# Bucketed attention with two gated layers on one core: first head's maxima by a product, hash products in two parts, zero products in the first waits, a new written sequence

## The chip, the cores and the metric

The kernel runs on one core of a Trainium2 chip. The metric is the time of one execution in device microseconds. The core has a matrix engine (PE in the profile, with its weight loads as PEld), three engines that work on whole tiles (DVE, ACT, POOL) and SP, which here only issues transfers. ACT issues some transfers too; SP and ACT each have a queue of their own, in which a transfer that has to wait holds up everything behind it.

## The reference

Three layers follow each other. The first is attention in which a query sees only the keys of its own hash bucket; the second is a gated layer (`moe`), the third a layer with one of eight experts for each token (`moe2`). The change is in the first.

```python
q_bits = (np.einsum('bhsd,dk->bhsk', q, proj) > 0)     # 6 bits, k likewise
q_bucket = np.sum(q_bits * powers, axis=-1)
mask = q_bucket[:, :, :, None] == k_bucket[:, :, None, :]
scores = np.where(mask, scale * q @ k.T, -1e9)
scores = scores - np.max(scores, axis=-1, keepdims=True)
attn = np.exp(scores); attn = attn / (np.sum(attn) + 1e-09)
out = attn @ v                 # 2 x 8 heads, 768 positions, 64 wide, float32
```

## The kernel before

**Work.** The sixteen heads are taken two at a time: eight pairs `i`, with heads `j` 0 and 1 of each. For a pair, q and k are loaded (`l`), turned by six PE transposes each (`tt`, line 636), and split into a leading part (`tc`, ACT, line 645) and a rest (`td`, DVE, line 658; for the last pair two products and an ACT copy, `tl`). Products with the hash matrix PRJ give the signed dots (`pk`/`pb`, line 667), one DVE comparison makes bits of them (`bi`, line 672; for the first pair four smaller ones, `bh`, line 688). Leading parts, rests and bits are copied into the operand tile T of each head, by transfers (`d0`, `d1`, `d2`, `e2`), for the first pair partly by ACT and POOL copies (`c0`, `c1`).

**Maxima and scores.** For each head six blocks of 128 queries are multiplied with all keys, bits included (`sm`, line 720), and DVE takes the row maxima (`sx`, line 728). The maxima are turned by a PE transpose (`mk` step 0, line 735), limited from below on DVE (step 1, line 738) and sent by a transfer on ACT's queue into one row of T (step 4, line 748); steps 2 and 3 mark the queries without a key. With that row in T the score products (`sc`, line 757) come out with the maximum already subtracted. ACT takes the exponential (`ex`, line 765), POOL the rest of it in 16 bits (`pl`, line 776), and three products a block with v give the output (`pv`, lines 792 to 794; `pu` adds the unmatched queries). `va`, `vx`, `vs` scale v, `sv` and `mvm` make its mean, `ho` divides.

**Start.** DVE zeroes PRJ (`prz`, line 910), fills rows and constants (`rows`, lines 553 to 567), then constants from the identity tile (`vm1`, lines 581 to 586; `nid`, line 912), then PRJ (`prj`, lines 541 to 550, when `proj` has landed). PE makes two columns from the rows (`cols`, line 572). The identity tile is made by POOL ahead of everything. POOL zeroes T (`z`) and other tiles and makes constants (`const`).

**Order.** `ORDER` holds one string for each engine (PE, ACT, DVE, POOL, SP), and each engine executes its steps in just that order. `Plan.order` only merges the five strings with the dependencies; the costs in `add(...)` enter there. PSUM has three large buffers ("S") for `tt`, `pb`, `sm` and `sc`; k and q of one pair have one raw buffer each, so the next pair's load waits for this pair's `tt`. In the kernel before, the loads of pair 1 and of its v also wait for the first pair's bits `d1.0.0`:

```python
add(SP, 1300, ("l", i, nm), load_qk, (i, nm), [("l", i - 1, nm)] + [("d1", 0, 0)] * (i == 1), ...)
add(SP, 1270, ("lv", i), load_v, (i,), [("lv", i - 1)] * (i > 0) + [("d1", 0, 0)] * (i == LV0), ...)
```

Of the kernel before, what the change touches and what calls it, by code (L numbers as in the profile page):

```python
# [1728 lines left out]
```

## Time and profile before

| | |
|---|---|
| three runs | 786.21, 787.86 (median), 791.44 us |
| profiled execution, own time | 787.57 us |
| its span, first to last instruction | 785.9 us |
| busy in the span | PE 740.8, PEld 623.6, DVE 464.5, POOL 425.1, ACT 377.5 us |
| mean granted clock of PE | 0.971 |

The span lacks 1.7 us of the execution's own time. Busy time of PE counts a product from its issue to its modelled end, and products overlap. Attention takes the first 244 us of the span, and the gated layers the rest. In the rows, `x6` is a count, a bracket gives the idle time of the engine just before the row and what ended it, and an engine's name with q (SPq, ACTq) is its transfer queue. The granted clock is 1.00 for 2.4 GHz and 0.50 for 1.2 GHz; the record has its first change at 19.5 us.

### The profile page before, as it was taken

The page shows a single profiled execution, that of the slowest core. Times are in us where ns is not written, and L with a number is a line of the kernel's source. Part 1 is how long each engine was busy: PE and PEld are TensorE (multiplying, and loading weights), DVE is VectorE, ACT ScalarE, POOL GpSimd, SP SyncE. Part 2 cuts the span into 40 slices and gives each one's busy share as a digit, 9 for nine tenths or more (in the row PEclk, how much of TensorE's full clock was granted, in tenths as well). Part 3 has the DMA queues.
Part 4 walks back from the last instruction along what each step waited for, and adds up shares of the span by engine and source line. Part 5 has one row for each costly group of instructions (what it writes and reads, how often), then busy time and mean ns, then how long its engine had stood idle before and what let it go on. Part 6 is the DMA issues. An engine that isn't in the chain of part 4 may idle for free.

```text
span 785.9 us, 14028 instructions
## 1 busy us (share of the span) xinstructions
PE 740.8 (94%) x5322; PEld 623.6 (79%) x5322; DVE 464.5 (59%) x869; ACT 377.5 (48%) x612; POOL 425.1 (54%) x378
## 2 busy tenths in 40 slices
...
GB/s 110 205 171 163 152 109 118 114 142 130 122 30 81 108 161 107 164 158 81 1 55 1 0 44 12 14 67 1 80 160 338 335 289 220 218 180 181 23 25 21
DMA packets 109235, 92.17 MB, mean 117 GB/s; under 512 B 45699, under 2 KB 90851, under 8 KB 109164
## 3 DMA queue, kind: packets, MB, share of 16 engines
...
## 4 chain that ended last, share of the span: by engine, by line
PE 81%; DVE 6%; DMA 6%; issue 3%; SPq 1%; ACT 1%; POOL 1%; ACTq 0%; POOLq 0%; DVEq 0%
PE pg L1084 23%; PE pg L1564 11%; PE pss L757 7%; PE psm L720 4%; PE po L1138 4%; PE po L1140 4%; PE po L1139 4%; PE po L1578 3%; PE po L1576 3%; PE po L1577 3%; DMA T<-bits 2%; PE po L792 2%; PE po L793 2%; PE po L794 2%; PE pt L339 1%
## 5 line engine op out<-in xcount | busy, mean ns | idle before, releaser
L776 POOL TENSOR_TENSOR Pl<-Pe 128x768 f16<-128x768 f32 x90 | 133.4, 1503 | 41.3 <-ACT Pe L765 36.8
L456 POOL TENSOR_TENSOR wgl<-r,wgh 128x512 fp32r<-128x512 f32 x64 | 83.5, 1310 | 79.6 <-ACT wgh L466 73.8
L765 ACT ACTIVATE Pe<-pss,ebias 128x768 f32<-128x768 f32 x96 | 84.5, 901 | 76.3 <-PE pss L757 47.7
L728 DVE TENSOR_REDUCE m<-psm 128x1 f32<-128x768 f32 x96 | 90.4, 953 | 34.8 <-PE psm L720 33.1
L757 PE MATMUL pss<-T 128*128 128x256 f32 (+1 forms) x384 | 88.6, 363 | 2.6 <-DMA T<-mT 2.3
L757 PEld LDWEIGHTS pss<-T 128*128 128x128 f32 x384 | 67.1, 198 | 17.5 <-issue 3.4
L1103 POOL TENSOR_TENSOR wol<-wy_o,woh 128x512 fp32r<-128x512 f32 x36 | 48.8, 1358 | 57.8 <-ACT woh L466 57.8
L1103 POOL TENSOR_TENSOR wgl<-wy_g,wgh 128x512 fp32r<-128x512 f32 x29 | 39.0, 1344 | 75.8 <-ACT wgh L466 69.7
L456 DVE TENSOR_TENSOR wvl<-r,wvh 128x512 fp32r<-128x512 f32 x64 | 48.6, 759 | 48.2 <-ACT wvh L466 45.1
L1564 PE MATMUL pg<-xh,wgh 128*128 128x256 f32 x256 | 73.2, 287 | 0.7 <-ACT xh L342 0.7
L1564 PE MATMUL pg<-xh,wgl 128*128 128x256 f32 x256 | 72.5, 283 | 0.0
L1564 PE MATMUL pg<-xl,wgh 128*128 128x256 f32 x256 | 72.5, 283 | 0.0
L1116 DVE TENSOR_TENSOR si<-pg,si 128x512 f32<-128x512 f32 x30 | 20.7, 689 | 78.8 <-PE pg L1084 76.3
L720 PE MATMUL psm<-T 128*128 128x512 f32 x192 | 56.4, 388 | 8.3 <-DMA T<-bits 6.6
L792 PE MATMUL po<-VS,Pe 128*128 128x65 f16 x576 | 62.1, 196 | 0.0
L1103 POOL TENSOR_TENSOR wvl<-wy_v,wvh 128x512 fp32r<-128x512 f32 x29 | 40.2, 1388 | 40.2 <-ACT wvh L466 36.2
L1084 PE MATMUL pg<-xh,wgh 128*128 128x512 f32 x144 | 57.6, 400 | 4.3 <-ACT wgh L466 4.3
L794 PE MATMUL po<-VS,Pl 128*128 128x65 f16 x576 | 61.0, 193 | 0.5 <-POOL Pl L776 0.5
L793 PE MATMUL po<-VS,Pe 128*128 128x65 f16 x576 | 61.5, 195 | 0.0
L466 ACT CAST wgh<-r 128x512 fp32r<-128x512 f32 x64 | 39.7, 620 | 42.0 <-PE pg L1564 31.0
L1138 PE MATMUL po<-woh,hh 128*128 128x512 f32 (+1 forms) x148 | 58.8, 397 | 0.1
L792 PEld LDWEIGHTS <-Pe 128*128 128x128 bf16 x576 | 52.7, 97 | 7.6 <-issue 6.0
...
## 6 DMA issues: line engine op xcount, KB each, us to landing
r<-in_moe_w_dram SPq DMA_DIRECT2D x128, 256.0 KB
...
```

The costliest lines, as they stand in the source:

```text
L456: eng.tensor_tensor(out=lo, in0=y, in1=r32(hi), op=ALU.subtract)
L720: nc.tensor.matmul(pm[:, c], Tj[:, 0, 1, t * P:(t + 1) * P], Tj[:, 0, 0, c], start=True, stop=True)
L728: v_.tensor_reduce(out=d["m", j][:, t:t + 1], in_=d.pop(("pm", n)), axis=AX.X, op=ALU.max)
L757: nc.tensor.matmul(pss[:, c], Tj[:, a, 0, ks], Tj[:, a, 1, c], start=a == 0, stop=a == 1)
L765: nc.scalar.activation(d["p", j][0][:, kb], d.pop(("s", n)), AF.Exp, bias=ebias, scale=1.0 / math.sqrt(D))
L776: eng.tensor_tensor(out=Pl[:, kb], in0=Pe[:, kb], in1=leading(Pe, kb), op=ALU.subtract)
L792: nc.tensor.matmul(po, leading(Pe, kb)[:, ts], vf[:, 0], start=t == 0 and kb == 0, stop=False, skip_group_check=True)
L793: nc.tensor.matmul(po, leading(Pe, kb)[:, ts], vf[:, 1], start=False, stop=False, skip_group_check=True)
L1084: nc.tensor.matmul(pg, w_[:, dsl], x_[:, d], start=n == 0, stop=n == 3 * KD - 1)
L1103: nc.gpsimd.tensor_tensor(out=lo, in0=Y[(f, kind)], in1=r32(hi), op=ALU.subtract)
L1138: nc.tensor.matmul(pos[c, t][:, cols], d["hh"][:, tsl], wh[:, cols], start=first, stop=split, skip_group_check=split)
L1564: nc.tensor.matmul(ph, w_[:, dsl], x_[:, d], start=n == 0, stop=n == 3 * KD - 1)
```

## The change

It does nine things, all in attention.

1. `load_pj`: one transfer on ACT's queue, a broadcast over two halves, in place of one on SP and one on ACT.
2. The hash columns move by one, so that the row of maxima is the first of its group (partition 64 or 0), where one instruction can write it.
3. The first head's maxima: `row_first` limits them into column 64 of six zeroed blocks MZ (DVE, `mz.0.0`), multiplies each with a copy of the identity (PE, six products, `mz.0.1`), and copies row 64 of the result into T in two pieces (DVE 512 and ACT 256 elements, `mz.0.2`, `mz.0.3`). Steps 1 and 4 of `mk.0.0` go. MZ, the identity copy and the zeros lie in a part of `T[1][1]`, zeroed by POOL (`zz`) and DVE (`iz`); pair 1's `d2.1.1`, which writes there, waits for all of them.
4. The first pair's hash products in two parts: the two with the leading part (`ph`) right after `tc`, the one with the rest (`pk`, `pb`) after `td`.
5. Zero products of 128x512 (`WARM`): 4 ahead of `cols`, 4 and 3 ahead of `tt.0.k` and `tt.0.q`, 6 ahead of `sm.0.0`. `cols` now waits for `iz` too.
6. `TDA = (1, 4)`: pair 1's rests by two products each and an ACT copy, not on DVE.
7. The loads of pair 1 and of its v no longer wait for `d1.0.0`.
8. The planner's costs for transfers change, and a PE step that waits for a PE step no longer waits out a signal's time in it.
9. All five strings of `ORDER` are written anew, to the end of attention.

```diff
-LV0 = 1
+WARM = {("cols",): 4, ("tt", 0, "k"): 4, ("tt", 0, "q"): 3, ("sm", 0, 0): 6}
-TDA = (4,)
+TDA = (1, 4)
 ORDER = (
-    "cols tt.0.k tt.0.q pk.0 pb.0 sm.0.0 sm.0.4 sm.0.3 sm.0.1 vx.0.1 sm.0.5 sm.0.6 sm.0.2 mk.0.0.0 tt.1.k sm.0.9 sm.0.8 tt.1.q sc.0.0 sc.0.5 sm.0.10 "
-    "tt.2.k pb.1 sc.0.2 sm.0.11 sm.0.7 tt.2.q vx.1.1 mk.0.1.0 sc.0.1 sm.1.0 sm.1.3 vx.0.5 sm.1.1 sc.0.6 sc.0.4 sm.1.5 sc.0.7 vx.1.5 sc.0.11 sm.1.6 sc.0.3 "
+    "cols tt.0.k tt.0.q ph.0.0 pk.0 ph.0.1 pb.0 tt.1.k tl.1.k sm.0.0 sm.0.5 tt.1.q sm.0.2 tl.1.q sm.0.3 sm.0.1 sm.0.4 pb.1 mz.0.1 mk.0.0.0 sm.0.6 sm.0.10 "
+    "sm.0.7 sc.0.0 sm.0.11 vx.0.1 sm.0.9 sc.0.2 sm.0.8 sc.0.3 vx.1.1 sc.0.4 mk.0.1.0 sm.1.0 sc.0.5 sm.1.6 sc.0.1 vx.0.5 sm.1.3 tt.2.k sm.1.11 vx.1.5 "
...
-    "d1.1.0 ex.0.2 tc.2.q mk.0.1.4 ex.0.1 d1.1.1 vs.0.0 ex.0.6 ex.0.4 ex.0.7 ex.0.11 ex.0.3 ex.0.9 ex.0.10 va.1.0 ex.0.8 mk.1.0.4 mr.0.1 vs.1.0 d1.2.0 "
-    "tc.3.k mr.0.3 d1.2.1 mk.1.1.4 ex.1.0 va.1.1 ex.1.5 va.1.2 tc.3.q ex.1.6 ex.1.9 va.1.3 ex.1.8 ex.1.3 ex.1.2 ex.1.4 ex.1.1 ex.1.7 tc.4.k ex.1.10 tc.4.q "
+    "pj l.0.k l.0.q tc.0.k c0.0.0.0 tc.0.q c0.0.1.1 va.0.0 c0.0.0.1 tc.1.k td.1.k d1.0.1.1 tc.1.q td.1.q c0.0.1.0 va.0.2 va.0.1 mz.0.3 d1.1.0 d1.1.1 "
+    "ex.0.0 va.0.3 ex.0.2 ex.0.3 ex.0.4 mk.0.1.4 ex.0.5 ex.0.1 vs.0.0 tc.2.k tc.2.q vs.1.0 ex.0.6 ex.0.10 ex.0.8 va.1.0 mr.0.1 ex.0.7 ex.0.9 mr.0.3 "
+    "mk.1.0.4 va.1.1 va.1.2 ex.0.11 d1.2.0 d1.2.1 ex.1.0 tc.3.k ex.1.2 ex.1.4 mk.1.1.4 tc.3.q ex.1.1 va.1.3 ex.1.5 ex.1.6 ex.1.10 ex.1.3 ex.1.7 ex.1.8 "
...
-    "prz rows vm1 nid prj bc td.0.k td.0.q bh.0.0.0 bh.0.1.0 bh.0.0.1 bh.0.1.1 sx.0.0 sx.0.3 vx.0.0 sx.0.4 sx.0.5 sx.0.1 sx.0.2 sx.0.6 mk.0.0.1 vx.0.2 "
+    "vm1 rows iz nid prz prj td.0.k bc td.0.q bh.0.1.0 bh.0.0.0 bh.0.0.1 bh.0.1.1 sx.0.0 sx.0.5 sx.0.2 sx.0.3 sx.0.1 sx.0.4 vx.0.0 mz.0.0 bi.1 sx.0.6 "
+    "mz.0.2 sx.0.10 sx.0.7 sx.0.11 sx.0.9 mk.0.0.2 vx.1.0 sx.0.8 vx.1.2 vx.0.2 vx.1.3 vx.0.3 mk.0.1.1 sx.1.0 vx.0.4 sx.1.6 vx.1.4 vx.0.6 mk.0.1.2 sx.1.3 "
...
-    "ho.5.1.2 sx.7.1 n5.2 vs.7.1 sx.7.11 mk.7.0.2 mk.7.0.1 sx.7.10 sx.7.7 sx.7.9 n5.3 sx.7.8 mk.7.1.2 ho.6.0.0 mk.7.1.1 ho.6.0.1 pl.7.0 w0.v.2 ho.6.0.2 "
-    "w0.v.3 w0.v.4 pl.7.4 ho.6.1.0 pl.7.6 pl.7.2 ho.6.1.1 ho.6.1.2 pl.7.10 pl.7.8 ho.7.0.0 ho.7.0.1 ho.7.0.2 w0.g.2 w0.g.3 w0.g.4 w0.v.6 w0.g.6 ho.7.1.0 "
+    "mk.6.1.2 vs.7.1 sx.7.2 sx.7.6 mk.7.0.2 mk.7.0.1 sx.7.8 sx.7.7 sx.7.9 sx.7.10 sx.7.11 ho.6.0.0 ho.6.0.1 ho.6.0.2 pl.7.0 w0.g.2 mk.7.1.1 w0.g.3 w0.g.4 "
+    "mk.7.1.2 ho.6.1.0 ho.6.1.1 ho.6.1.2 pl.7.2 pl.7.6 pl.7.4 w0.v.2 pl.7.10 pl.7.8 w0.v.3 w0.v.4 ho.7.0.0 ho.7.0.1 ho.7.0.2 w0.v.6 ho.7.1.0 w0.g.6 "
...
-    "ev.0 z.0.0 z.0.1 ut0 z.1.0 c1.0.0.1 c1.0.1.0 c1.0.1.1 z.1.1 c1.0.0.0 const sv.0.2 pl.0.0 sv.0.0 mk.0.0.3 sv.0.3 pl.0.5 sv.0.1 pl.0.2 pl.0.1 pl.0.4 "
+    "z.0.1 c1.0.0.0 ut0 zz z.0.0 z.1.1 z.1.0 c1.0.1.1 sv.0.1 ev.0 c1.0.1.0 c1.0.0.1 sv.0.2 ev.1 const sv.0.0 sv.0.3 pl.0.2 mk.0.0.3 pl.0.0 pl.0.4 pl.0.3 "
...
-    "l.0.k.0 pj.0 l.0.q.0 lv.0 e2.0.0 d1.0.1.0 e2.0.1 lv.1 l.1.k l.1.q lv.2 l.2.k lv.3 l.2.q d0.1.0 lv.4 d0.1.1 d2.1.1 d2.1.0 lv.5 l.3.k lv.6 d0.2.0 l.3.q "
+    "l.0.k.0 l.0.q.0 lv.0 l.1.k l.1.q lv.1 d1.0.1.0 l.2.k lv.2 e2.0.0 e2.0.1 lv.3 d0.1.0 d0.1.1 l.2.q lv.4 d2.1.1 lv.5 l.3.k lv.6 d2.1.0 d0.2.0 l.3.q lv.7 "
...
+        def idle_zero():
+            v_.memset(r32(spare[:, 0, 0:256]), 0.0)
+
+        def max_zero():
+            nc.gpsimd.memset(r32(MZ), 0.0)
+            nc.gpsimd.tensor_copy(identr, ident)
+
+        def keep_warm(dst, *key):
+            for _ in range(WARM.get(key, 0)):
+                nc.tensor.matmul(dst[:, 0:512], idle[:, 0:P], idle, start=True, stop=True)
...
+        def dots_first(a, part):
+            if part == 0:
+                st[0]["pd", a] = bank("pd")
+            pd = st[0]["pd", a]
+            hi, lo, w = ((1, 0, 1), (2, 3, 0))[a]
+            for c in pieces:
+                for n in range(2 - part):
+                    nc.tensor.matmul(pd[:, c], PRJ[:, w, n], st[0]["hl"][:, lo if part else hi, c],
+                                     start=(part, n) == (0, 0), stop=part == 1, skip_group_check=True)
...
+        def row_first(step):
+            d = st[0]
+            if step == 0:
+                v_.tensor_scalar(out=MZ[:, :, 64], in0=d["m", 0], scalar1=-PEN / 2, scalar2=None, op0=ALU.max)
+            elif step == 1:
+                d["pz"] = bank("pz")
+                for t in range(NT):
+                    nc.tensor.matmul(d["pz"][:, t * P:(t + 1) * P], MZ[:, t], identr, start=t % 4 == 0, stop=t in (3, NT - 1),
+                                     skip_group_check=True)
+            else:
+                c = pieces[step - 2]
+                dst, src = T[0][0][64:65, 0, 1, c], d["pz"][64:65, c]
+                v_.tensor_copy(dst, src) if step == 2 else nc.scalar.copy(dst, src)
...
-        add(PE, 580, "cols", mask_cols, (), ("rows",), -99, "V")
+        add(PE, 580, "cols", mask_cols, (), ("rows", "iz"), -99, "V")
...
-                    add(SP, 1300, ("l", i, nm), load_qk, (i, nm), [("l", i - 1, nm)] + [("d1", 0, 0)] * (i == 1),
+                    add(SP, 1300, ("l", i, nm), load_qk, (i, nm), [("l", i - 1, nm)],
...
-            add(SP, 1270, ("lv", i), load_v, (i,), [("lv", i - 1)] * (i > 0) + [("d1", 0, 0)] * (i == LV0), MLT[b] + LV[i % HP], bw=1970)
+            add(SP, 1270, ("lv", i), load_v, (i,), [("lv", i - 1)] * (i > 0), MLT[b] + LV[i % HP], bw=1850)
```

## Rows read from the trace of the kernel before

**Rows 1.** Busy time by stage: us, PE, PEld, DVE, ACT, POOL, PEclk, DMA share, GB/s
```profile
40.00:50.00 10.00, 6.30 (x19) 5.15 (x20) 4.87 (x7) 3.47 (x5) 3.75 (x4) 0.67 0.63 131
50.00:60.00 10.00, 10.00 (x48) 7.21 (x48) 6.78 (x11) 6.65 (x9) 8.04 (x7) 0.99 1.17 218
...
200.00:210.00 10.00, 10.00 (x106) 8.73 (x106) 5.44 (x8) 5.48 (x7) 5.79 (x5) 0.83 0.52 168
```

**Rows 2.** The chain that ended last, first 60 us: start, us, what
```profile
19.17 4.55 DMA kraw<-in_k_dram
...
35.70 1.07 DVE bits L672
...
37.66 5.91 DMA T<-bits
...
43.70 1.62 PE psm L720 x4
```

**Rows 3.** Timeline, first 5 us: start, us, engine, line, what
```profile
0.89 0.06 DVE L251 MEMSET ebias<- 128x1 f32 x1 [0.89 <-PEq L1713]
...
2.62 1.00 PE L572 MATMUL pc<-one,rowc 1*128 1x1 f32 x4 [2.62 <-DVE one L564]
...
2.91 1.37 POOL L577 MEMSET T<- 64x1536 f32 x1
3.00 0.16 DVE L581 TENSOR_TENSOR diag<-ident 38x6 f32<-38x6 f32 x1 [0.27 <-POOL ident masks.py:199]
...
3.22 1.28 DVE L586 CAST VB<-ident 38x6 f16<-38x6 f32 x4
```

**Rows 4.** Timeline, 5 to 36 us: the same products early and late, and the path to the scores
```profile
5.25 1.51 PE L636 MATMUL pt<-ident,kraw 128*128 128x128 f32 x6 [1.62 <-DMA kraw<-in_k_dram]
...
9.90 4.21 PE L667 MATMUL pd<-HL,PRJ 128*128 128x512 f32 x12 [0.71 <-DVE HL L658]
...
16.67 0.96 DVE L728 TENSOR_REDUCE m<-psm 128x1 f32<-128x768 f32 x1
...
23.90 0.76 ACTq L748 DMA_DIRECT2D T<-mT  x1
...
27.70 1.54 PE L636 MATMUL pt<-ident,qraw 128*128 128x128 f32 x6 [1.05 <-DVE m L728]
...
28.90 2.91 PE L757 MATMUL pss<-T 128*128 128x512 f32 x8
...
33.29 2.36 PE L667 MATMUL pd<-HL,PRJ 128*128 128x512 f32 x12
```

**Rows 5.** Groups on DVE, first 16 us, forms apart: busy us, mean ns, idle before
```profile
L688 DVE TENSOR_SCALAR T<-pd,bc 13x768 fp32r<-13x768 f32 x2 | 2.2, 1080 | 1.2 <-PE pd L667 1.2
...
L658 DVE TENSOR_TENSOR HL<-pt,HL 128x768 fp32r<-128x768 f32 x2 | 1.9, 958 | 0.2 <-ACT HL L645 0.2
...
L910 DVE MEMSET PRJ<- 128x512 f32 x1 | 0.5, 485 | 0.1
```

**Rows 6.** Groups on ACT, first 50 us, forms apart
```profile
L645 ACT CAST HL<-pt 128x768 fp32r<-128x768 f32 x6 | 4.8, 799 | 13.0 <-PE pt L636 12.0 <-DMA qraw<-in_q_dram 0.9
...
L679 ACT CAST T<-HL 64x768 fp32r<-64x768 f32 x4 | 3.3, 825 | 5.6 <-POOL onesb L308 5.6
```

**Rows 7.** Busy time of two short stretches, columns as in rows 1
```profile
8.00:10.00 2.00, 1.29 (x7) 0.89 (x5) 1.71 (x7) 1.24 (x2) 0.00 (x0) 1.00 0.04 8
...
20.00:22.00 2.00, 0.93 (x4) 0.60 (x4) 1.86 (x3) 0.00 (x0) 0.00 (x0) 1.00 1.28 219
```

**Rows 8.** What PE waited for, 150 to 270 us: us in total, times, longest
```profile
PE pg L1084 <- ACT wgh L466: 4.3, 2, 3.8
```

**Rows 9.** Timeline, 190 to 206 us: ACT's queue and the scores behind it
```profile
195.72 4.77 ACTq L709 DMA_DIRECT2D T<-bits  x4
...
199.82 2.36 PE L757 MATMUL pss<-T 128*128 128x512 f32 x8 [2.29 <-DMA T<-mT]
```

**Rows 10.** Timeline, 62 to 65 us: pair 1's first score products
```profile
63.98 0.93 PE L757 MATMUL pss<-T 128*128 128x512 f32 x4
```

More of the change, by code (lines that the diff above doesn't have):

```diff
@@ L188, in order @@
                 heapq.heappush(events, (end + self.WAIT[e], 1, n))
+                if e == PE:
+                    heapq.heappush(events, (end, 2, n))
             if not events:
@@ L195, in order @@
                     continue
-                done += 1
-                for b in steps[n][7]:
-                    room[b].append(self.slots.get((self.taker(n, b), b), 0))
+                if ended == 1:
+                    done += 1
+                    for b in steps[n][7]:
+                        room[b].append(self.slots.get((self.taker(n, b), b), 0))
                 for m in after[n]:
+                    if (steps[n][0] == PE == steps[m][0]) != (ended == 2):
+                        continue
                     left[m] -= 1
@@ L516, in attention @@
         T = [[ea.tile([P, 2, 2, S], F32R, name=f"T{s}{j}") for j in range(2)] for s in range(TB)]
+        spare = T[1][1][:, 1]
+        idle, identr = r32(spare[:, 0, 0:256]).bitcast(BF16), spare[:, 0, 256:256 + P]
+        MZ = spare[:, 1].rearrange("p (t c) -> p t c", t=NT)
         VS = [tp.tile([P, NT, 2, 2 * D + 2], F16, name=f"VS{i}") for i in range(2)]
@@ L534, in attention, with load_pj @@
         vsc = [tp.tile([P, 1], F32, name=f"vsc{g}") for g in range(len(scaled))]
-        def load_pj(j):
-            (nc.scalar if j else nc.sync).dma_start(pj[64 * j:64 * j + 64, 0], proj)
+        def load_pj():
+            nc.scalar.dma_start(pj[:, 0], proj.unsqueeze(0).to_broadcast((2, D, NB)))
         def prj():
@@ L557, in mask_rows @@
                     c0 = row_of(j, w)
-                    v_.memset(rowc[:, 0, c0:c0 + MR], SPEN)
-                    m0 = c0 + NB if w == 0 else c0
+                    v_.memset(rowc[:, 0, c0 + 1:c0 + NR], SPEN)
+                    m0 = c0 + 1 + NB if w == 0 else c0 + 1
                     v_.memset(rowc[:, 0, m0:m0 + NB], -SPEN)
@@ L562, in mask_rows @@
                     if w == 1:
-                        v_.memset(rowc[:, :, c0 + MR:c0 + NR], -1.0)
+                        v_.memset(rowc[:, :, c0:c0 + 1], -1.0)
             v_.memset(one1, 1.0)
@@ L570, in mask_cols @@
             pc = ps_v.tile([P, 512], F32, name="pc", tag=plan.tag("V"))
+            keep_warm(pc, "cols")
             for i in range(2):
@@ L718, in smax @@
             pm = bank("psm")
+            keep_warm(pm, "sm", i, n)
             for c in pieces:
@@ L905, in first_hi @@
             W0[kind] = split_hi(Y[(0, kind)], kind)
-        for j in range(2):
-            add((SP, ACT)[j], 620, ("pj", j), load_pj, (j,), (), -997, bw=20)
+        add(ACT, 620, "pj", load_pj, (), (), -1999, bw=-1500)
+        add(DVE, 170, "iz", idle_zero, (), (), -1000)
+        add(POOL, 900, "zz", max_zero, (), [("z", 0, 1)], -90)
         add(DVE, 325, "prz", lambda: v_.memset(r32(PRJ), 0.0), (), (), -98)
-        add(DVE, 2000, "prj", prj, (), [("pj", 0), ("pj", 1), "prz"], -97, lock=True)
+        add(DVE, 2400, "prj", prj, (), ["pj", "prz"], -97, lock=True)
         add(DVE, 120, "nid", lambda: v_.tensor_scalar(out=nident, in0=ident, scalar1=-1.0, scalar2=None, op0=ALU.mult), (), (), -90, lock=True)
         add(DVE, 1200, "rows", mask_rows, (), (), -99)
-        add(PE, 580, "cols", mask_cols, (), ("rows",), -99, "V")
+        add(PE, 580, "cols", mask_cols, (), ("rows", "iz"), -99, "V")
         add(DVE, 150, "bc", lambda: v_.tensor_copy(bc, st[0].pop("pc")[:, 0:2]), (), ("cols",), -99, "", "V")
@@ L975, in attention @@
                     for w, nm in enumerate("kq"):
-                        add(ACT, 750, ("c0", i, j, w), place_first, (j, 0, w), [("tc", i, nm)], r0 + PT[n][1] + 0.1 + 0.01 * j)
-                        add(POOL, 1200, ("c1", i, j, w), place_first, (j, 1, w), [("tc", i, nm) if w == 0 else ("td", i, nm)], -99)
+                        add(ACT, 830, ("c0", i, j, w), place_first, (j, 0, w), [("tc", i, nm)], r0 + PT[n][1] + 0.1 + 0.01 * j)
+                        add(POOL, 830, ("c1", i, j, w), place_first, (j, 1, w), [("tc", i, nm) if w == 0 else ("td", i, nm)], -99)
@@ L988, in attention @@
+                add(ACT if i < QA else SP, 1650, ("d1", i, j), place, (i, j, 1), [("bi", i)] + war, r0 + PT[n][3] + 0.01 * j, bw=-2200 if i < QA else 240)
+                add(SP, 1270, ("d2", i, j), place, (i, j, 2), hl + war + ([("fz", 0)] + ["cols" if len(key) == 1 else key for key in WARM]) * ((i, j) == (1, 1)), r0 + PT[n][4] + 0.01 * j, bw=4400)
             add(None, 0, ("fh", i), None, (), [("pk", i)] * (i == 0) + [("pb", i)] + [(d, i, j) for d in ("d0", "d2") for j in range(2)], 0, "", "HL")
@@ L1005, in attention @@
                 ring = ACT if i < QA else SP
-                for m, (e, ns) in enumerate(((PE, 110), (DVE, 270), (DVE, 270), (POOL, 180), (ring, 640))):
-                    add(e, ns, ("mk", i, j, m), setm, (i, j, m), [("mk", i, j, (0, 0, 0, 2, 1)[m])] + (["ut0"] + [("pu", i - NUR // 2, j)] * (i >= NUR // 2)) * (m == 2) if m else red, pr + 0.001 * (m in (2, 3)),
-                        ("V", "MK", "", "", "")[m], "", bw=0 if m < 4 else -1800 if i < QA else 20)
-                add(None, 0, ("fv", i, j), None, (), [("mk", i, j, 1), ("mk", i, j, 2)], 0, "", "V")
@@ L1010, in attention @@
-                add(None, 0, ("fm", i, j), None, (), [("mk", i, j, 0)], 0, "", "M")
-                add(None, 0, ("fk", i, j), None, (), [("mk", i, j, 4)], 0, "", "MK")
+                for m, (e, ns) in enumerate(((PE, 110), (DVE, 270), (DVE, 270), (POOL, 180), (ring, 760))):
+                    if (i, j) == (0, 0) and m in (1, 4):
+                        if m == 1:
+                            add(DVE, 140, ("mz", i, 0), row_first, (0,), red + ["zz"], pr)
+                            add(PE, 360, ("mz", i, 1), row_first, (1,), [("mz", i, 0)], pr, "S")
+                            add(DVE, 640, ("mz", i, 2), row_first, (2,), [("mz", i, 1)], pr)
+                            add(ACT, 450, ("mz", i, 3), row_first, (3,), [("mz", i, 1)], pr)
+                            add(None, 0, ("fz", i), None, (), [("mz", i, 2), ("mz", i, 3)], 0, "", "S")
+                        continue
+                    add(e, ns, ("mk", i, j, m), setm, (i, j, m), [("mk", i, j, (0, 0, 0, 2, 1)[m])] + (["ut0"] + [("pu", i - NUR // 2, j)] * (i >= NUR // 2)) * (m == 2) if m else red, pr + 0.001 * (m in (2, 3)),
+                        ("V", "MK", "", "", "")[m], "", bw=0 if m < 4 else -1700 if i < QA else 20)
@@ L1012, in attention @@
+                first = (i, j) == (0, 0)
+                top = ("fz", i) if first else ("mk", i, j, 4)
+                add(None, 0, ("fv", i, j), None, (), [("mk", i, j, 2)] if first else [("mk", i, j, 1), ("mk", i, j, 2)], 0, "", "V")
+                add(None, 0, ("fm", i, j), None, (), [("mk", i, j, 0)] + [("mz", i, 0)] * first, 0, "", "M")
+                if not first:
+                    add(None, 0, ("fk", i, j), None, (), [("mk", i, j, 4)], 0, "", "MK")
                 for m in range(NT):
```

30 lines of the change are left out of this document (15 added, 15 removed), and 86 rows, old and new, of the table ORDER.

## The prediction

> **What bounds the kernel now.** I read the windows first. From 50 us on PE is busy for nearly all of every ten microseconds until the end of attention, at the full clock; in the ten before that it is not: 6.30 us busy, at a mean clock of 0.67 [rows 1]. So what attention gains is what its start gains: work that reaches the full stage earlier ends earlier, and what is added there counts one for one. The chain of waits says what holds the start: not the arithmetic of the first head, but pair 1. Its k leaves late and lands 4.55 us after its issue at 19.17; its bits are made at 35.70; their transfer takes 5.91 us, and only at 43.70 do pair 1's maxima products begin [rows 2]. I therefore take that moment, the first `sm.1`, as the mark by which both kernels are compared, and follow the new order to it on the trace's own time axis.
>
> **The first head: later.** DVE now begins with `vm1`, which waits for the identity; before, that wait ended at 3.00, after two small memsets and one T memset on POOL [rows 3]. In the new order one T memset stands there, so I put it at 2.7. The four small casts of `vm1` took until 4.5 beside a 1.37 us POOL memset [rows 3]; POOL now stands still until `tc.0.k`, so I give the casts the 0.16 us of the small addition beside them [rows 3], and `vm1` 0.65 us: 3.4. `rows` took 1.2 us before: from DVE's first instruction at 0.89 to the release of `cols` at 2.62 [rows 3], less the PRJ memset of 0.485 [rows 5]; `iz` is half such a memset. So DVE frees `cols` at 4.9, not at 2.62. Only then does PE start, and its order is fixed: four zero products, `cols` (1.0 us [rows 3]), four zero products, and then k's transposes, whose data landed at 5.25 [rows 4]. A zero product has no row; the nearest is the hash product of the same width: twelve of them, nine 512-column widths, took 4.21 us early and 2.36 late [rows 4], so 0.26 to 0.47 us for one. I take 0.47, since PE has been idle, and the transposes at 1.51 us early [rows 4]: 4.9 + 3.8 + 1.0 + 1.5 = 11.2 if the low level lasts; as the level may rise on the way, I take 10.5 for the end of `tt.0.k`, against 6.8 before. The zero products hide nothing there, they stand in the way. `proj` on ACT's queue and the columns moved by one I cost at nothing: DVE reaches `prj` at about 5.6 and needs some 2.5 us for it, and the first hash product cannot start before `tc.0.k` at 11.3, so 3 us cover it; without that cover its lateness would go into `ph` one for one.
>
> From 10.5: `tc.0.k` 0.80, `c0` 0.83, `tc.0.q` 0.80 [rows 6] to 13.0, `td.0.q` 0.96 [rows 5] to 14.0. The hash products in two parts pay here: the leading parts run during `tc` and `td`, so that a third of them is left after `td`; but four bit comparisons of 1.08 us [rows 5] follow on DVE anyway, so this is worth about 0.7 us. The second of them needs `z.0.0`, which POOL now reaches after `c1` (0.82), `ut0` (0.8), `zz` (0.9, half a T memset and a copy): at 15.2 with its 1.37. The comparisons end at 17.4 for the first head; six zero products lie ahead of `sm.0.0`, of which half are hidden: first reduction at about 18.9, against 16.67 [rows 4]. The start of the reductions loses 2.2 us.
>
> **The maxima by a product: nothing.** Before, mT left at 23.90 and the scores began at 28.90, but what they waited for was not it: PE stood behind q's transposes of pair 1, which waited for a buffer that a reduction freed at 27.70 [rows 4]. In the new order the six reductions end at 24.8 and `mz.0.0` at 25.0, but `bi.1` (1.08) and `sx.0.6` (0.96) stand ahead of the copy `mz.0.2`. The copy has no row: between 0.16 (38x6 [rows 3]) and 1.08 us (13x768 [rows 5]); I take 0.72 by its 512 columns. With `bi.1` ending at 26.5, `sc.0.0` begins at 28.2, and I count the exchange itself at 0; its bounds are -0.7, by the two starts of the scores, and +1 if `mz.0.3` comes late behind `va` on ACT.
>
> **Pair 1: earlier.** Its k leaves when `tt.0.k` ends, at 10.5 instead of shortly before 19.17 [rows 2], into transfer engines that moved 8 GB/s from 8 to 10 us [rows 7]. With 0.7 us of issue and the 4.55 us of before [rows 2] it lands at 15.8, q at 17.5. Both are turned between the first head's products; the rests come from two products and an ACT copy of 0.80 each, and `pb.1` is done at about 25.4. `bi.1` ends at 26.5 instead of 36.8 [rows 2]. ACT then issues four bit transfers of 0.8 us without a break; with the 5.91 us of landing [rows 2] counted from the second, the bits are there at 33. On DVE, head 1's remaining reductions (five of 0.96, one copy 0.72) after 28.2 end at 33.7, and PE's order has `mk.0.1.0` ahead of `sm.1.0`. Two paths end together: `sm.1.0` at 34.0 against 43.70, a gain of 9.7 us.
>
> Not yet done at the mark are pair 2's transposes, 1.5 us in the early rate, which the kernel before had behind it; the number of score products done is four in both. That leaves 8.2. What the mark does not show: at 43.70 PE had stood for 4 us and ran at half clock to 50 us; if it does not fall this time, up to half of those 6.5 us, 3.3, come on top [rows 1]; I take 0, as reductions and exponentials feed PE there.
>
> **The end of attention.** The first gate weight is now converted ahead of the last output steps. PE waited for it twice, 3.8 us at the longest [rows 8], of which 0.9 right at the change of layer; I take that 0.9, and keep 0 and 2 as ends. For the rest of the new sequence I have no term: its work is the same, and its waits can go either way by some 4 us, as the stall at 195 to 204 us shows [rows 9].
>
> **Sum.** Against the profiled execution, 787.57 us: -9.7 + 1.5 - 0.9 = -9.1, so 778.5 us. That execution lies 0.3 below the median shown.
>
> **Rivals.** First, the transfers become the bound. With both loads of pair 1 pulled ahead, SP's order has 22 blocks of 393 KB up to `d2.1.0`, three more than before, which `sc.1.0` needs. At 219 GB/s [rows 7] that is 39.5 us, from 2.3 us on and with 5 us of forced gaps: 47, against a need at about 54, the mark plus the 20 us that lay between it and pair 1's first scores at 63.98 [rows 10]. At the 131 GB/s of the stage from 40 to 50 us [rows 1] it would be 73; halfway, at 175 GB/s, 57 plus a little to land, a wait of 4: 782.5 us. For it: the chain runs over three such landings [rows 2]; against it: the 131 stands for a stage in which nothing was queued. The Trainium skill, "DMA: Bandwidth & Descriptors", section "Issuing engines are not separate DMA queues", says that transfers from SP and ACT end on the same 16 engines and interleave; by that, bits on ACT's queue would get no path of their own beside the loads. The trace agrees: the bits took 5.91 us beside the loads [rows 2].
>
> Second, the clock stays low through the first head. All of `tt.0`, `ph`, `pb.1` then runs at the early rates: `tt.0.k` 0.7 later, q's transposes and three zero products 1.3, six zero products 1.2 (each by the early less the late price), and of the 1.9 that `pb.1` grows by 0.4 uncovered: 3.6 us, 782.1. For it: the products at 9.90 still took 4.21 us, though PE had done k's transposes from 5.25 on [rows 4]. The Trainium skill, "TensorE: Matmul & The Clock Gate", section "What's actually happening", has the slow level as the default, which activity releases; by that the zero products would bring the full rate by q's transposes. The trace agrees with the default, in that these early rows are slow; none of its stretches shows work on zeros.
>
> Third, slower: ACT's queue. Where four bit transfers are issued in a row (4.77 us), the maxima wait behind them and PE's scores stand for 2.29 us [rows 9], after which the clock is down for some 3.4 us (0.83 over ten [rows 1]), at half worth: 4 us in all. The new ACT order has such rows for pairs 1 and 2 and splits pair 7's, which speaks against it; but each pair has the maxima on this queue. It decides from the third such stall on; with four, 16 - 9 = +7: 794.6 us.
>
> Fourth, more: no half clock from 34 us on (-3.3) and no stall at 195 us: 773 or below.
>
> **Chances.** Forecast 0.45, transfers 0.20, low clock 0.12, ACT's queue 0.09, more 0.14. The range from 770 to 789 leaves out the slower case and little else. A measurement of this kernel can tell about 1%, 7.9 us. Below 780: three in five of the forecast (0.28), the fourth case and a little of the others: 0.47. Above 795.7: 0.07. The rest, 0.46, is within 1%.
>
> **What would show it.** `cols` at about 5 and `tt.0.k` ending near 10.5 in the timeline; first reduction near 19; k of pair 1 issued near 10.5; scores near 28; first `sm.1` near 34; PE full from about 40 in the windows. Wrong if the first transposes are not late, if `sm.1` stands behind bits beyond 38, or if PE shows new waits between 60 and 240 us.

## The result, and the profile after

The changed kernel takes 777.29 us (median of four, 776.77 to 779.23), the kernel before 787.04 in the same runs (784.98 to 791.44): 9.75 us less, ratio 0.987 with an interval from 0.983 to 0.992. The profiled execution took 777.31 us, its span is 775.6 us, PE's mean clock 0.981. The forecast was 778.5.

First the windows, columns as in [rows 1], which the first, second and last line answer:

```profile
40.00:50.00 10.00, 10.00 (x96) 7.65 (x97) 9.49 (x14) 7.83 (x12) 8.24 (x7) 1.00 1.07 203
50.00:60.00 10.00, 9.38 (x139) 8.14 (x139) 7.94 (x13) 5.42 (x9) 8.72 (x10) 1.00 0.80 170
150.00:160.00 10.00, 7.27 (x114) 5.97 (x112) 9.58 (x12) 3.61 (x4) 9.13 (x8) 0.99 0.55 114
160.00:170.00 10.00, 9.79 (x99) 8.72 (x100) 7.14 (x19) 5.43 (x7) 2.89 (x2) 0.84 0.46 101
200.00:210.00 10.00, 9.71 (x142) 8.33 (x141) 7.67 (x10) 5.52 (x7) 8.35 (x7) 1.00 0.01 2
```

From 40 to 50 us PE is now busy throughout at the full clock (6.30 us at 0.67 before), and the stretch around 200 us runs at 1.00 instead of 0.83. But from 150 to 170 us there is a hole of 2.7 us and a stretch at half clock that the kernel before does not have: it had 1.00 there, and 9.24 and 10.00 us busy.

Then the timeline of the changed kernel; it answers [rows 2 to 4], and its last three lines are the hole:

```profile
4.84 1.89 PE L596 MATMUL pc<-T 128*128 128x512 bf16 x4 [4.84 <-DVE T L588]
6.66 1.01 PE L584 MATMUL pc<-one,rowc 1*128 1x1 f32 x4
7.60 1.89 PE L596 MATMUL pt<-T 128*128 128x512 bf16 x4
9.28 1.49 PE L660 MATMUL pt<-ident,kraw 128*128 128x128 f32 x6
10.56 1.49 PE L596 MATMUL pt<-T 128*128 128x512 bf16 x3
...
10.80 1.23 SPq L629 DMA_DIRECT2D kraw<-in_k_dram  x2
...
11.84 1.38 PE L660 MATMUL pt<-ident,qraw 128*128 128x128 f32 x6
...
14.05 4.22 POOL L600 MEMSET T<- 64x1536 f32 x3
...
15.57 0.82 PE L660 MATMUL pt<-ident,kraw 128*128 128x128 f32 x6
...
17.82 1.47 PE L596 MATMUL psm<-T 128*128 128x512 bf16 x6
...
19.67 2.69 DVE L763 TENSOR_REDUCE m<-psm 128x1 f32<-128x768 f32 x3 [0.19 <-PE psm L755]
...
26.00 0.78 PE L792 MATMUL pz<-T 128*128 128x128 f32 x6
...
27.36 4.00 ACTq L743 DMA_DIRECT2D T<-bits  x4
...
29.11 1.00 PE L806 MATMUL pss<-T 128*128 128x512 f32 x4 [0.20 <-DVE T L797]
...
35.13 0.27 PE L770 MATMUL pT<-ident,m 128*6 128x128 f32 x1
...
154.96 4.31 POOL L825 TENSOR_TENSOR Pl<-Pe 128x768 f16<-128x768 f32 x3
...
155.23 4.07 DVE L377 TENSOR_SCALAR nri<-nrb 128x4 int32<-128x4 int32 x1
...
160.21 2.93 PE L806 MATMUL pss<-T 128*128 128x512 f32 x8 [2.94 <-DVE m L763]
```

PE begins at 4.84 with zero products and turns k from 9.28, q from 11.84. Pair 1's k leaves at 10.80 and is turned at 15.57, its bits leave at 27.36. The first `sm.1` follows the transpose at 35.13 without a wait, so the mark of the prediction lies at 35.15 instead of 43.70. In the hole one DVE operation on 128x4 numbers takes 4.07 us, as long as three POOL instructions beside it, and PE stands for 2.94 us behind the reduction that follows.

To see where the time went, I counted every matrix product by the columns that it moves, from the start on, and looked up when both kernels had done the same amount; zero products, the extra products for rests (pairs 1 and 7) and those of the maxima's row are left out, so that both totals are equal (a product counts when it ends; counted when it starts, no entry moves by more than 0.3).

| done before at (us) | 30 | 60 | 150 | 160 | 170 | 190 | 210 | 250 | 300 | 560 | 600 |
|---|---|---|---|---|---|---|---|---|---|---|---|
| changed kernel earlier by | 4.4 | 9.8 | 10.3 | 11.7 | 7.4 | 8.5 | 12.7 | 11.8 | 11.3 | 11.3 | 10.1 |

The start gains 9.8, the hole costs 4.3, the stall at 195 us that is gone [rows 9] gives back 4.2, the end of attention loses 1.4, the change to the last layer 1.2. Below, "lead" is this number.

### The profile page after: what moved, and what is told of

It reads as the page before. It is cut to its first block, busy times and chain, and to the rows that moved or that the text cites. A ratio compares the mean times of both kernels' runs of the same rounds, so it can differ in the third digit from the quotient of the medians.

```text
span 775.6 us, 14106 instructions
## 1 busy us (share of the span) xinstructions
PE 735.8 (95%) x5349; PEld 618.7 (80%) x5349; DVE 464.5 (60%) x869; ACT 379.0 (49%) x615; POOL 427.6 (55%) x380
## 4 chain that ended last, share of the span: by engine, by line
PE 83%; DVE 5%; DMA 3%; issue 3%; POOL 2%; ACT 2%; SPq 0%; ACTq 0%; POOLq 0%
PE pg L1146 23%; PE pg L1626 11%; PE pss L806 8%; PE po L1200 4%; PE po L1202 4%; PE po L1201 4%; PE psm L755 4%; PE po L1640 4%; PE po L1638 3%; PE po L1639 3%; PE po L841 2%; PE po L842 2%; PE po L843 2%; PE pt L346 1%; PE pt L660 1%
## 5 line engine op out<-in xcount | busy, mean ns | idle before, releaser
L806 PE MATMUL pss<-T 128*128 128x256 f32 (+1 forms) x384 | 83.9, 351 | 5.3 <-DVE m L763 2.9
L806 PEld LDWEIGHTS pss<-T 128*128 128x128 f32 x384 | 64.6, 191 | 20.7 <-DVE m L763 3.4
L841 PE MATMUL po<-VS,Pe 128*128 128x65 f16 x576 | 58.8, 195 | 0.0
L843 PE MATMUL po<-VS,Pl 128*128 128x65 f16 x576 | 57.9, 193 | 0.9 <-POOL Pl L825 0.9
L1146 PE MATMUL pg<-xh,wgl 128*128 128x512 f32 x144 | 57.3, 398 | 1.5 <-POOL wgl L1165 1.2
L842 PE MATMUL po<-VS,Pe 128*128 128x65 f16 x576 | 58.2, 194 | 0.0
L1631 DVE SCALAR_TENSOR_TENSOR ehl<-pg,ehh 128x256 fp32r<-128x256 f32 x64 | 27.1, 424 | 51.6 <-ACT ehh L1630 51.6
L1146 PE MATMUL pg<-xl,wgh 128*128 128x512 f32 x144 | 57.7, 401 | 0.2 <-DVE xl L353 0.2
```

What stands on the lines that cost most here:

```text
L806: nc.tensor.matmul(pss[:, c], Tj[:, a, 0, ks], Tj[:, a, 1, c], start=a == 0, stop=a == 1)
L841: nc.tensor.matmul(po, leading(Pe, kb)[:, ts], vf[:, 0], start=t == 0 and kb == 0, stop=False, skip_group_check=True)
L842: nc.tensor.matmul(po, leading(Pe, kb)[:, ts], vf[:, 1], start=False, stop=False, skip_group_check=True)
L843: nc.tensor.matmul(po, Pl[:, kb, ts], vf[:, 0], start=False, stop=False, skip_group_check=True)
L1146: nc.tensor.matmul(pg, w_[:, dsl], x_[:, d], start=n == 0, stop=n == 3 * KD - 1)
```

## Experiments

All are compared with the kernel before in the same runs; its medians there were 786.0 to 786.6 us. The changed kernel's 777.29 is from the first runs, in which the kernel before stood 0.5 to 1.0 us higher; so a difference to it is uncertain by about 1 us, and one of less than that says nothing.

### The zero products

```diff
-WARM = {("cols",): 4, ("tt", 0, "k"): 4, ("tt", 0, "q"): 3, ("sm", 0, 0): 6}
+WARM = {}
```

> The changed kernel without its 17 zero products, order kept. Theory A (they pay by the clock): in the changed kernel the granted clock is 1.0 from 13.0 us on without a break to 159.8; without them PE does little before 10 us, the level rises later, near 19.5 us as in the kernel before, and falls again in the stretches 23 to 33 and 43 to 50 us, so that the 3 us which the first transposes gain (k's end near 7.5 instead of 10.8) are more than eaten: 780 to 784 us. Theory B (they only stand in the way, as the prediction had it): the first head is 3 us earlier, first reduction near 16.5 instead of 19.7, and it stays so: 774 us.

774.36 us (773.79 to 775.75), ratio 0.984 [0.980, 0.988]: 2.9 us faster than with them. Theory B, and theory A falls with its ground: the clock is 1.00 in each ten microseconds from 20 to 50 here too, and the first hash products, twelve in 2.85 us from 10.03 on, are hardly slower than with zeros (2.75 us from 12.98 on; [rows 4] have 4.21 early and 2.36 late). Its timeline:

```profile
4.40 1.01 PE L584 MATMUL pc<-one,rowc 1*128 1x1 f32 x4 [4.40 <-DVE one L575]
7.28 1.51 PE L660 MATMUL pt<-ident,kraw 128*128 128x128 f32 x6 [1.87 <-DMA kraw<-in_k_dram]
8.87 1.51 PE L660 MATMUL pt<-ident,qraw 128*128 128x128 f32 x6
10.03 2.85 PE L701 MATMUL pd<-HL,PRJ 128*128 128x512 f32 x12
...
16.70 2.80 DVE L763 TENSOR_REDUCE m<-psm 128x1 f32<-128x768 f32 x3
```

q's transposes start 3.0 us earlier, and so does the first reduction. The run shows something else: now k's transposes wait 1.87 us for data that in the kernel before were there at 5.25 [rows 4]. The zero products had hidden that.

### Pair 1 late again

Loads, turning, hash products and bits of pair 1 back behind the first head's work (here SP's and PE's strings; ACT's and DVE's follow):

```diff
-l.0.k.0 l.0.q.0 lv.0 l.1.k l.1.q lv.1 d1.0.1.0 l.2.k lv.2 e2.0.0 e2.0.1 lv.3
+l.0.k.0 l.0.q.0 lv.0 d1.0.1.0 e2.0.0 e2.0.1 l.1.k l.1.q lv.1 l.2.k lv.2 lv.3
-pb.0 tt.1.k tl.1.k sm.0.0 sm.0.5 tt.1.q sm.0.2 tl.1.q ... sm.0.4 pb.1 mz.0.1 mk.0.0.0 sm.0.6 sm.0.10
+pb.0 sm.0.0 sm.0.5 sm.0.2 ... sm.0.4 mz.0.1 mk.0.0.0 tt.1.k tl.1.k sm.0.6 sm.0.10 tt.1.q tl.1.q ... sm.0.9 pb.1
```

> The changed kernel with pair 1's loads behind the first head's placing on SP, and its turning, hash products and bits in the places that they had before. Theory A (the early start of pair 1 carries the gain): the first maxima product of pair 1 goes from 35.2 to about 42 us, and the time to 784 us. Theory B (the high clock from 13 us on carries it): pair 1 has time to spare, the first maxima product comes by 38, and the time stays below 780.

801.66 us (800.12 to 802.69), far more than either theory. The edit had a flaw, which ACT's timeline shows:

```profile
34.11 0.84 ACT L868 ACTIVATE junk<-X 128x768 f32<-128x768 f32 x1 [12.71 <-DMA X<-in_v_dram]
...
36.04 0.36 ACT L797 CAST T<-pz 1x256 fp32r<-1x256 f32 x1
```

A sum over v waits 12.71 us for its load, and the copy of the first head's maxima stands behind it in ACT's order; the scores begin at 43.85. So this run prices two things. The second one has the copy ahead of these sums, and the loads as in the kernel before:

```diff
-lv.0 d1.0.1.0 e2.0.0 e2.0.1 l.1.k l.1.q lv.1 l.2.k lv.2 lv.3
+lv.0 d1.0.1.0 e2.0.0 e2.0.1 lv.1 l.1.k l.1.q lv.2 l.2.k lv.3
-c0.0.1.0 va.0.2 va.0.1 mz.0.3 tc.1.k td.1.k tc.1.q td.1.q ex.0.0 va.0.3 ex.0.2 d1.1.0 d1.1.1
+c0.0.1.0 mz.0.3 tc.1.k td.1.k va.0.1 tc.1.q td.1.q ex.0.0 va.0.2 va.0.3 d1.1.0 d1.1.1
```

> The changed kernel with pair 1 late again, as in the run before of this kind, but without its flaw: there the copy of the first head's maxima on ACT stood behind sums over v that waited 12.7 us for late loads; here the copy stands ahead of them and the loads of v and of pair 1 have the order that they had in the kernel before. Theory A (the early start of pair 1 carries the gain): the first maxima product of pair 1 at 42 to 44 us, against 35.2, and 784 to 788 us. Theory B (it does not, the 801.7 of the run before came from ACT's queue alone): below 780.

791.71 us (788.29 to 794.66), ratio 1.006 [1.004, 1.009]: 14.4 us more than the changed kernel. The mark in PE's timeline, and the window from 30 to 40 us, columns as in [rows 1]:

```profile
46.93 1.01 PE L755 MATMUL psm<-T 128*128 128x512 f32 x2 [2.10 <-ACT Pe L814]
...
30.00:40.00 10.00, 8.86 (x29) 6.68 (x28) 5.36 (x6) 5.75 (x9) 8.31 (x27) 0.52 0.81 170
```

The first `sm.1` comes at 46.93, later than I had expected and 3 us later than in the kernel before: the rest of the new order is written for an early pair 1. Theory A by direction, and more than its size. The 14.4 us are not the price of the late pair alone: from 30 to 40 us PE runs at 0.52, where the changed kernel has 1.00, and the run does not separate the two. What it does show is that the new order without the early pair 1 is no faster than the kernel before.

### The loads alone

The kernel before, with one part of the change:

```diff
-l.0.k.0 pj.0 l.0.q.0 lv.0 e2.0.0 d1.0.1.0 e2.0.1 lv.1 l.1.k l.1.q lv.2
+l.0.k.0 pj.0 l.0.q.0 lv.0 l.1.k l.1.q e2.0.0 d1.0.1.0 e2.0.1 lv.1 lv.2
```

> The kernel before with one part of the change alone: the loads of pair 1's k and q right behind the first head's on SP, all else as it was. Theory A (the load is only the first link, PE's written order holds pair 1 back just the same, its transposes stand behind the first head's maxima): k is there by 11 us instead of 23.7 and waits; the first maxima product of pair 1 moves by 1.5 us at most: 786 us. Theory B (the late load was the cause): pair 1 moves by 8 us: 779 us.

786.72 us, ratio 1.001 [0.998, 1.003]: nothing. Theory A; SP's queue and PE in the timeline:

```profile
6.85 1.23 SPq L606 DMA_DIRECT2D kraw<-in_k_dram  x2
...
23.70 1.48 PE L636 MATMUL pt<-ident,kraw 128*128 128x128 f32 x6
...
27.51 1.54 PE L636 MATMUL pt<-ident,qraw 128*128 128x128 f32 x6 [1.05 <-DVE m L728]
...
43.53 1.62 PE L720 MATMUL psm<-T 128*128 128x512 f32 x4 [4.54 <-DMA T<-bits]
```

k leaves from 6.85 on instead of 18.43 (the first of its two issues; [rows 2] show the second) and, with the 4.55 us of landing of [rows 2], lies there for some eleven microseconds; PE turns it at 23.70, behind the first head's maxima, and the first `sm.1` waits for bits until 43.53 (43.70 before). An early load is worth only what the order of the engine that uses it takes up. The run also shows that the dependency on `d1.0.0`, which it still has in its source, held nothing: the loads left more than 5 us ahead of the first pair's first comparison (12.24). It was SP's written order that held them, so point 7 of the change does nothing by itself.

### The first head's maxima

The transfer of before in place of `row_first`, at the same places of the orders:

```diff
-pb.1 mz.0.1 mk.0.0.0      (PE)      -va.0.1 mz.0.3 d1.1.0     (ACT)
+pb.1 mk.0.0.0             (PE)      +va.0.1 mk.0.0.4 d1.1.0   (ACT)
-vx.0.0 mz.0.0 bi.1 sx.0.6 mz.0.2 sx.0.10   (DVE)
+vx.0.0 mk.0.0.1 bi.1 sx.0.6 sx.0.10        (DVE)
```

> The changed kernel with the first head's maxima brought into their row by a transfer on ACT's queue, as in the kernel before; its product, its two copies and the first clamp are left out. Theory A (as the prediction had it, the exchange is worth nothing, bounds -0.7 to +1): scores from about 29, 777 us. Theory B (the product saves the landing of the transfer): the row is written about 26.8 + 0.8 + 3 = 30.6 us, the scores begin 1.5 to 2 us later, 779 us.

779.94 us (777.55 to 780.46): 2.7 us more, though the two ranges overlap; the lead is 6.2 at 60 us against 9.8, and 7.4 against 10.1 at 600. Theory B and more. The timeline and the window from 30 to 40 us, columns as in [rows 1] (the changed kernel has 8.98 us busy at 1.00 there):

```profile
26.45 0.77 ACTq L783 DMA_DIRECT2D T<-mT  x1
...
32.11 1.62 PE L806 MATMUL pss<-T 128*128 128x512 f32 x4 [4.01 <-DMA T<-mT]
...
30.00:40.00 10.00, 7.69 (x32) 6.09 (x33) 4.55 (x11) 4.43 (x6) 5.75 (x9) 0.68 0.91 177
```

The transfer leaves at 26.45, the scores wait 4.01 us for it, start 3.0 us later than with the product, and after that wait the clock is down: 0.68 in this window.

### The hash products undivided

```diff
-tt.0.q ph.0.0 pk.0 ph.0.1 pb.0
+tt.0.q pk.0 pb.0
```

> The changed kernel with the first head's hash products undivided: all six of k behind the rest of k, all six of q behind the rest of q. Theory A (worth 0.7 us, as the prediction had it): q's six, 1.3 us at the high clock, follow the rest of q at 15.1 instead of two of them; bits and first reduction 0.7 to 0.9 later, 778 us. Theory B (the first comparison on DVE waits for POOL's zeroed T in any case, so that nothing is lost): 777.3.

776.40 us (775.50 to 777.21), 0.9 less than with them divided, lead 10.2 at 60 us against 9.8: theory B by its number, though not by its reason. Its q transposes, the first six hash products, the first comparison on DVE and the first reductions:

```profile
11.83 0.82 PE L660 MATMUL pt<-ident,qraw 128*128 128x128 f32 x6
...
12.66 1.32 PE L691 MATMUL pd<-HL,PRJ 128*128 128x512 f32 x6
...
14.51 1.07 DVE L722 TENSOR_SCALAR bits<-pd,bc 13x768 fp32r<-13x768 f32 x1
...
19.71 2.69 DVE L763 TENSOR_REDUCE m<-psm 128x1 f32<-128x768 f32 x3 [0.80 <-PE psm L755]
```

The comparison begins 0.03 us behind q's rest (13.52, 0.96 us), which stands ahead of it in DVE's own order, and waits for no product: k's six were done by 14.0. In this profile q's transposes already ran at the full rate (0.82 us, 1.38 in the changed kernel), and all that hangs on them came 0.6 us earlier; the first reduction did not (19.71 and 19.67). Ahead of it PE's order has pair 1's rest products and six zero products, until 19.3, and DVE waits 0.80 us for the product behind them.

### The hole at 155 us

The operation of 4.07 us is the first guess of the norm's root (`n1.2`). Once it goes behind six other DVE steps, once three steps forward:

```diff
-mk.5.0.2 n1.2 sx.5.8 ho.4.0.0 n1.3 sx.5.7 ho.4.0.1 n1.4 ho.4.0.2 sx.5.10 n1.5
+mk.5.0.2 sx.5.8 ho.4.0.0 sx.5.7 ho.4.0.1 ho.4.0.2 sx.5.10 n1.2 n1.3 n1.4 n1.5
```

> The changed kernel with one 128x4 operation of the first norm (the guess, 4.07 us at 155.23 beside three POOL instructions, alone 0.16) some seven DVE steps later, the two steps that hang on it with it. Theory A: that wait stops the reductions, so PE stands at 157 to 163 us and its clock falls; moved to where POOL pauses it takes under 1.5 us, PE has no hole there, the clock stays at 1.0: 773 to 774 us. Theory B: the hole comes from PE's own order or from POOL being late, and opens wherever the operation stands: 777 us.

```diff
-n1.1 sx.5.9 sx.6.0 mk.5.0.2 n1.2 sx.5.8
+n1.1 n1.2 sx.5.9 sx.6.0 mk.5.0.2 sx.5.8
```

> The changed kernel with the guess of the first norm three DVE steps earlier, right behind the step that it needs, at 152.7 us, beside POOL instructions that follow each other without a gap until 159.3. Theory A (a small DVE operation waits for the POOL instruction that runs, no longer): it takes 1.4 to 1.6 us, PE's hole goes, 773 to 775 us. Theory B (it waits until POOL has nothing left to start): 6 us or more, the hole stays or grows, 777 to 780 us.

Later: 772.18 us (771.39 to 773.94), 5.1 less than the changed kernel. Earlier: 771.54 (771.31 to 772.77), 5.7 less. DVE and window of the first:

```profile
157.88 0.16 DVE L377 TENSOR_SCALAR nri<-nrb 128x4 int32<-128x4 int32 x1
...
150.00:160.00 10.00, 10.00 (x116) 8.37 (x112) 8.23 (x18) 5.53 (x7) 7.20 (x6) 1.00 0.70 151
```

and DVE and POOL of the second:

```profile
150.18 2.89 POOL L825 TENSOR_TENSOR Pl<-Pe 128x768 f16<-128x768 f32 x2
...
151.71 1.39 DVE L377 TENSOR_SCALAR nri<-nrb 128x4 int32<-128x4 int32 x1
```

Where POOL pauses the operation takes 0.16 us; beside POOL it waits 1.39 and ends 0.03 after POOL's row does. PE has no hole in either. In the kernel before, the same operation stood among four POOL rows that followed each other, and waited out only the one that ran, which ended at 167.20:

```profile
166.78 0.45 DVE L370 TENSOR_SCALAR nri<-nrb 128x4 int32<-128x4 int32 x1
```

So a single step of 0.16 us, put in a bad place, cost over half of what the start had gained. In all five other runs of the new order that left it in its place it took 4.04 to 4.07 us.

### Three edits at once

No zero products, the guess later, and proj's load behind the halves of k and q:

```diff
-pj l.0.k l.0.q tc.0.k
+l.0.k l.0.q pj tc.0.k
```

> The changed kernel with three edits: no zero products, the first norm's guess some seven DVE steps later, and proj's load behind the first halves of k and q on ACT's queue instead of ahead of them. Theory A (the three add up): 2.9 and 5.1 us from the runs without zeros and with the guess later, and of the 1.9 us for which PE waited for k's data in the run without zeros about 1.3, since the hash products then wait for proj: k's transposes start at 5.4 to 6.0 instead of 7.28, 768 us. Theory B (proj comes as much too late as k comes early, and holds the hash products): 769.3. Theory C (the gain of the later guess hangs on how DVE and POOL happen to meet, and is gone when the start moves): 773 to 774.

777.00 us (776.02 to 777.92): none of the three theories, and 9 us from the sum. k's transposes do start at 5.36. But proj lands at 8.60, and its splitting on DVE falls beside POOL's memsets. DVE's groups from 3 to 17 us (busy us, mean ns, idle before), then PE's first hash product in the timeline:

```profile
L560 DVE CAST PRJ<-pj 64x6 fp32r<-64x6 f32 x8 | 5.5, 693 | 0.0
...
L561 DVE TENSOR_TENSOR PRJ<-pj,PRJ 64x6 fp32r<-64x6 f32 x8 | 1.3, 161 | 0.3
...
15.38 4.14 PE L701 MATMUL pd<-HL,PRJ 128*128 128x512 f32 x12 [6.72 <-DVE PRJ L560]
```

Eight casts take 693 ns on average instead of 162 (four of them 1.15 to 1.31 us), and the hash products wait 6.72 us for them. The lead at 60 us is 6.7.

### The parts together

No zero products and the guess later; proj stays first:

> The changed kernel without zero products and with the guess of the first norm later; proj's load stays first on ACT's queue. Theory A (the two are far apart in time and add up; in the run of three edits it was the late proj that ate them, since its copies on DVE fell beside POOL's memsets and took 1.2 us each instead of 0.16): 777.3 - 2.9 - 5.1 = 769.3 us. Theory B (the later guess only helps when the start has this one timing): 774.

771.31 us (770.03 to 773.66). The lead at 60 us is 12.7, as without zeros alone (12.5), and there is no hole; of the 8.0 us of the sum 6.0 are in the median, 7.3 in the profiled run, which is the fastest of the five (770.03). Then proj in two halves, as the kernel before loads it (their places in the orders, on SP behind k's first half and on ACT first, are left out here):

```diff
-            nc.scalar.dma_start(pj[:, 0], proj.unsqueeze(0).to_broadcast((2, D, NB)))
+            (nc.scalar if j else nc.sync).dma_start(pj[64 * j:64 * j + 64, 0], proj)
```

> The run without zeros and with the later guess, and proj loaded in two halves on the two queues as in the kernel before (on SP behind k's first half, on ACT first), where k was there at 5.25 and q at 7.67 instead of 7.28 and 8.87. Theory A (the start is then bound by k and q): k's transposes at 5.4, q's at 7.7, first reduction 1.2 us earlier, 768.1 us. Theory B (proj's copies end only when POOL has begun its work at 7.8 us, two or three of them take 1.2 us each, and the hash products start no earlier than at 10): 769.3 to 770.

769.46 us (767.62 to 775.02), ratio 0.979 [0.976, 0.983]: the fastest of all, 7.8 us under the changed kernel. PE and DVE:

```profile
5.33 1.54 PE L660 MATMUL pt<-ident,kraw 128*128 128x128 f32 x6
...
7.42 1.51 PE L660 MATMUL pt<-ident,qraw 128*128 128x128 f32 x6 [0.55 <-DMA qraw<-in_q_dram]
...
8.59 2.86 PE L701 MATMUL pd<-HL,PRJ 128*128 128x512 f32 x12
...
15.12 2.66 DVE L763 TENSOR_REDUCE m<-psm 128x1 f32<-128x768 f32 x3
```

k at 5.33, q at 7.42, first reduction at 15.12: 1.4 us earlier than with the broadcast, and the lead at 60 us is 14.0. Theory A by its rows; the median lies in the range of theory B, and the ranges of the two versions overlap. With the hash products undivided on top of that:

> The run before of this list and the first head's hash products undivided. Theory A (the division is worth nothing, as in the changed kernel, where the undivided ones came out at 776.4 against 777.3): within 0.7 us of the run before. Theory B (with k and q earlier, q's six products stand between its rest and the comparison): 1 us more.

771.04 us (769.25 to 773.91), lead 12.7: theory B by its numbers. The rows here:

```profile
7.78 1.51 PE L660 MATMUL pt<-ident,qraw 128*128 128x128 f32 x6 [0.90 <-DMA qraw<-in_q_dram]
...
9.67 4.02 PE L691 MATMUL pd<-HL,PRJ 128*128 128x512 f32 x12 [0.37 <-DVE HL L682]
...
12.00 1.07 DVE L722 TENSOR_SCALAR bits<-pd,bc 13x768 fp32r<-13x768 f32 x1 [0.87 <-PE pd L691]
```

The comparison comes 1.2 us later than with the division (10.80). Of that, 0.36 is q, which landed later in this profile, and 0.87 a wait for k's products, which ran at the early rate: at the full rate the six take 1.32 us, as in the other undivided run, and would have ended at 11.0, ahead of q's rest (11.13). With the division and the early rate there is no such wait (the run before the two halves, comparison at 12.00 behind q's rest). So in this start the division is worth up to 0.9 us while the clock is low and nothing once it is up, and the two profiles differ in that (twelve products in 2.86 and in 4.02 us). In the changed kernel it is worth nothing.

## Why the prediction came out right, step by step

The time was met within 1.2 us, in part by luck. The start gave 9.8 us against 8.2 forecast; behind it the table has movements of up to 4.3 us in both directions, none of them forecast with its size, and they happen to cancel to 0.3. One sign that the prediction itself named as showing it wrong came too: PE has a new wait between 60 and 240 us, the 2.94 us of the hole, which hangs on DVE and POOL; no rival named them.

**First head later: right, a little short.** Forecast against trace: zero products from 4.9 and 4.84, end of `tt.0.k` 10.5 and 10.77, first reduction 18.9 and 19.67. `cols` came at 6.66, about where its sum had put it; the "about 5" among its signs left out the four zero products ahead. The zero products ran at the slow price, 1.89 us for four. That they "hide nothing there, they stand in the way" is shown by the run without them: of the 6.7 us of their rows, 2.9 counted.

**Proj at no cost: the step failed, unseen.** "`proj` on ACT's queue and the columns moved by one I cost at nothing" looked at the hash products alone, which had their cover. What the broadcast delayed was the load behind it: k's data at 7.28 instead of 5.25. The zero products covered that in turn; in the last version the two halves are worth 1.3 us of lead. Issuing the broadcast took 1.18 us against 0.61 for one half, which is 0.6 of the 2.0 us; where the rest comes from no run here shows. The cover that I named for `prj` was real: where proj came late, the first hash product waited 6.72 us.

**Hash products in two parts: 0.7 forecast, nothing measured** (0.9 us the other way). The four comparisons on DVE were named as its limit, but the first of them hung on DVE's own rest of q, and the first reduction on PE's order, so that nothing was left at all.

**The maxima by a product: the size was wrong.** "I count the exchange itself at 0" compared with the kernel before, where something else held the scores. In the new order the transfer would have been last: 2.7 us, the low clock behind its wait included. The scores, forecast at 28.2, began at 29.11. The term belonged in the sum, against a comparison within the new order.

**Pair 1: right.** Forecast against trace: k issued 10.5 and 10.80, bits made 26.5 and 27.28, mark 34.0 and 35.15; a gain of 8.55 instead of 9.7, less pair 2's transposes. The four bit issues took 4.00 us instead of the 3.2 assumed, but the mark did not wait for them. In the other path to the mark the sum counts the copy's 0.72 twice, in 28.2 and in 33.7; the last reduction, 33.0 without it, ended at 34.68. That the new start needs the early pair 1 is shown by the run that makes it late; how much of the gain is the pair's own is not, as that run's clock was down as well. That the loads alone do nothing is shown.

**The half clock from 43 us: taken as 0, came.** Pair 2's transposes, 0.82 and 0.88 us, are still to be done at the mark: 8.55 - 1.7 = 6.9. The lead at 60 us is 9.8; most of the 2.9 between is the stretch from 40 to 50 us in the windows (counted by columns the lead goes from 7.4 at the old mark, 43.70, to 9.4 at 50), with 3.3 as the upper end that the prediction gave.

**End of attention: wrong in sign.** The wait for the gate weight fell from 4.3 [rows 8] to 3.5 us, about as forecast, though the 0.9 at the change of layer is in no row: [rows 8] leave 0.5 for it, and that wait is gone. But the lead fell by 1.4 between 210 and 300 us. In the rows PE now waits 0.9 and 0.6 us for POOL in the last output products, where it had 0.5 before; what else is in it I did not test. The 1.2 lost at the change to the last layer appears in waits for gathered rows (4.2 against 3.3 us for that step); its cause stays open.

**The rest of the sequence: no term, ±4.** It held both: -4.3 in the new hole, +4.2 from the old stall. The hole is shown by two runs.

**Rivals.** Transfers: PE waits for no load between 60 and 240 us. Low clock: the early products were slow to 13 us, then full (q's transposes from 11.84 took 1.38 us, those of pair 1's k from 15.57 on 0.82). ACT's queue: one wait of 0.62 us for maxima at 56 us, no stall. The fourth, 773 or below, had both its conditions met, no half clock from 34 to 150 us and no stall at 195; it missed only by the hole, and without that the time is 772.
